# Second chunk's first layer ahead of the first chunk's second layer, with its activations in the room of v

## The chip, the core and the metric

The kernel runs on one core of a Trainium2 chip. Five engines work side by side, each through its own list of instructions in order: TensorE (PE in the profile; weight loads are PEld), VectorE (DVE), ScalarE (ACT), GpSimd (POOL) and SyncE (SP), which issues most transfers. The metric is the device time of one execution in microseconds.

## The reference

Block-sparse attention feeds a two-layer network. Cut to what matters:

```python
batch, n_heads, seq, head_dim = (4, 8, 768, 64)
block = 32                       # 24 blocks of keys, 3 random ones a row of blocks
mask  = neighbours (|i-j| <= 1) | first or last block row or column | 3 sampled blocks
scores = where(mask, q @ k.T / sqrt(64), -1e9)
attn = exp(scores - max); attn = attn / (sum + 1e-9)
x = (attn @ v)  -> 3072 tokens x 512
h = x @ w_in                     # 512 x 2048
g = where(h > 0, h, exp(min(h, 0)) - 1)
out = g @ w_out                  # 2048 x 512
```

All inputs and the output are float32.

## The kernel before

The 3072 tokens are 12 chunks of 256, three to a batch; t counts the chunks, b the batches. A chunk is made of two units of 128 tokens; the units of the first batch come in the order (0,1), (4,5), (2,3), those of the others (4,5), (0,1), (2,3). Unit 5 holds also the first and the last 32 tokens, which see all keys (the special rows, sp). Float32 values are kept as two float16 parts, hi and lo, and a product is taken as three float16 products.

For one chunk there is, first, attention: scores on TensorE (L479), the minimum on VectorE (L491), the exponential on ScalarE (L506), its hi part on ScalarE (L513) and lo part on VectorE (L518), a transposing transfer (L525), the product with v on TensorE (L538), normalisation on VectorE (L558), and transposes and splitting into xT (L340 on ScalarE, L343 on VectorE, one helper for q, k, v, p and x). Second, the first layer: eight pieces h{t}_{f} of 256 columns of w_in (`ffn_h`, L653), 24 matmuls each, and for each its activation: ScalarE L661 and L667, VectorE L671 (the last reader of the PSUM buffer), VectorE L675 (hi part of g), and the subtraction L678 (lo part of g), which is on VectorE for chunk 0 and on GpSimd for the others. Third, the second layer: o{t}_0 and o{t}_1 (`ffn_o`, L689), 48 matmuls each, scaled out by ScalarE (L697) and stored.

Buffers matter here. h and o share a pool of three PSUM buffers, so a fourth piece waits until the last reader of the first is done: L671 for an h, L697 for an o. The tile e of the activation has four buffers. The loads of q, k and v from memory share three staging buffers (tag st). The hi and lo parts of v of a batch lie in vN; they are stored to a scratch in memory (L418) from which the rows of each unit are gathered (SP L428 and L436, GpSimd L438). g lies in two tiles, gt, one set for all chunks.

The weights arrive as float32 and are decoded on the chip, in pieces: bits on ScalarE (L264, L267) and VectorE (L272, L275), the hi part on ScalarE (L287), the lo part on VectorE (L288). w_in (tiles wi) comes first and w_out (tiles wo) after; the last four pieces of w_out go through the small room wk, 512 columns at a time.

The order is set by a table of work: `st.at(step, rank, fn)` places each function; the steps are gone through from the first, by rank inside a step, and a scheduler that knows the tiles makes each engine's list of it. A chunk has 16 steps; `F0` = 12 is the first step of h0, `LEAD` = 22 the steps by which attention runs ahead of h. Chunk t has h at steps 12 + 16 t on and o eight steps after. `e0` is the step at which a chunk's attention starts; `unit`, `special`, `k_piece`, `v_piece` and `q_piece` place their work after it.

Of the kernel before, what the change touches and what calls it, by code (L numbers as in the profile page):

```python
# [13 lines left out]
ALU = mybir.AluOpType  # L14
# [25 lines left out]
def kernel(  # L40
# [26 lines left out]
    nc = tc.nc  # L67
# [15 lines left out]
    NFC = DFF // P  # L83
    NFP = NFC // 2
# [20 lines left out]
    st = Steps()  # L105
# [535 lines left out]

    hS, eS, oS = {}, {}, {}
    PROD_X = ((0, 0), (1, 0), (0, 1))
    gh, gl = ([gt[f // 4][:, f // 2 % 2, l, f % 2] for f in range(NFP)] for l in range(2))

    def ffn_h(t, f):
        ps = ps_f.tile([P, 2, CW], F32, tag="f", name=f"h{t}_{f}")
# [24 lines left out]
            e, hS.pop((t, f)), -IH * GS, e, op0=ALU.mult, op1=ALU.min)  # L672

    def ffn_act4(t, f):
        nc.vector.tensor_copy(gh[f], eS[t, f])  # L675

    def ffn_act5(t, f):
        (nc.gpsimd if t else nc.vector).tensor_tensor(  # L678
            gl[f], eS.pop((t, f)), gh[f], op=ALU.subtract)

    def ffn_o(t, m, part, nparts):
        if part == 0:
            oS[t, m] = ps_f.tile([P, DM], F32, tag="f", name=f"o{t}_{m}")
        o = oS[t, m]
        ms = slice(m * P, (m + 1) * P)
        for f in range(NFP * part // nparts, NFP * (part + 1) // nparts):
            for e in range(2):
                for n, (g, l) in enumerate(((gh, 0), (gh, 1), (gl, 0))):
                    nc.tensor.matmul(  # L689
                        o, lhsT=g[f][:, e, ms], rhs=wo[f // 2][:, f % 2, l, e],  # L690
                        start=(f == 0 and e == 0 and n == 0),
                        stop=(f == NFP - 1 and e == 1 and n == 2))

# [21 lines left out]
    NSTEP = 2 * NFP  # L715
    LEAD = 22
    F0 = 12

    def unit(s, b, u, qd, t, c0):
        lag = 4 if t == 1 else 6  # L720
        if qd == 0:
            st.at(s - (1 if t == 0 or s == F0 + 2 * NSTEP - LEAD else 3), 3.0,
                  lambda: gather_k(b, u, nc.scalar if t == 1 else nc.vector))
        st.at(s, 0, lambda: scores(b, u, qd))
        st.at(s, 5, lambda: sm_min(b, u, qd))
        st.at(s, 6, lambda: sm_exp(b, u, qd))
        if t == 0:
            st.at(s + 1, 0.5, lambda: turn_p(b, u, qd))
            st.at(s + 2, 1, lambda: attn_v(b, u, qd))
            if qd == 1:  # L730
                st.at(s + 2, 3.5, lambda: norm(b, u))
                st.at(s + 3, 0.6, lambda: turn_x(b, u, t, c0))
            return
        st.at(s + 1, 3.1, lambda: sm_hi(b, u, qd))
        st.at(s + 1, 3.2, lambda: sm_lo(b, u, qd))
        st.at(s + 2, 0.5, lambda: sm_T(b, u, qd))
        a = s + lag
        st.at(a, 1, lambda: attn_v(b, u, qd))
        if u == UL or qd == 1:
            st.at(a, 3.5, lambda: norm(b, u))  # L740
            st.at(a + 1, 7, lambda: turn_x(b, u, t, c0))

    def special(s, b, qd, t):
        st.at(s, 0, lambda: sp_scores(b, qd))
        for j in range(2):
            st.at(s, 5 + j, lambda j=j: sp_min(b, qd, j))
            st.at(s, 5.1 + j, lambda j=j: sp_exp(b, qd, j))
            st.at(s + 1, 3 + .3 * j, lambda j=j: sp_hi(b, qd, j))
            st.at(s + 1, 3.1 + .3 * j, lambda j=j: sp_lo(b, qd, j))
            st.at(s + 2, 0.5, lambda j=j: sp_T(b, qd, j))  # L750
        lag = 4 if t == 1 else 6
        st.at(s + lag, 1, lambda: sp_av(b, qd))
        if qd == NQ - 1:
            st.at(s + lag, 3.5, lambda: sp_x(b, t, P))
# [8 lines left out]
    def k_piece(s, b, c):  # L763
        staged.append((s, lambda: load_k(b, c)))
        st.at(s, 7.2, lambda: turn_k(b, c))
# [9 lines left out]
    for t, (b, us) in enumerate(chunks):  # L775
        f0 = F0 + t * NSTEP
        e0 = f0 - LEAD

        if t == 0:
            e0 = 0  # L780
            at, first = (1, 2, 3, 4), (1, 3)
        elif t == 1:
            e0 = f0 - NSTEP + 2
            at, first = (e0, e0 + 2, e0 + 3, e0 + 5, e0 + 6), (e0, e0 + 3)
        elif us[1] < UL:
            at, first = (e0, e0 + 4, e0 + 8, e0 + 12), (e0, e0 + 8)
        else:
            at, first = (e0, e0 + 3, e0 + 5, e0 + 8, e0 + 12), (e0, e0 + 5)
        if us[1] < UL:
            for n, s in enumerate(at):  # L790
                unit(s, b, us[n // 2], n % 2, t, P * (n // 2))
        else:
            unit(at[0], b, us[0], 0, t, 0)
            unit(at[1], b, us[0], 1, t, 0)
            special(at[2], b, 0, t)
            special(at[3], b, 1, t)
            unit(at[4], b, UL, 0, t, P + 64)
        for m, u in enumerate(us):
            s = first[m]
            if t == 0:  # L800
                continue
            q_piece(s - 3, b, u)

        opens = t == 0 or chunks[t - 1][0] < b
        for m, u in enumerate(us):
            s = e0 - 4 + 8 * m
            if t == 0:
                s = 2 * m
            elif t == 2 and m == 0:
                s += 3  # L810
            if opens:
                st.at(s, 0.2, lambda b=b, m=m, e=None if t or m else nc.gpsimd: edge_v(b, m, e))
            for i in range(blocks_in(u)):
                st.at(s + (i if t else 0), 0.3, lambda b=b, u=u, i=i: gather_v(b, u, i))
        if opens:
            st.at(at[0] - 1, 2.95, lambda b=b: ends_of_k(b))

        if opens and b + 1 < B:
            for n, (g, qd) in enumerate(PIECES):
                if t == 0:  # L820
                    k_piece(24 + 2 * n, b + 1, n)
                    v_piece(22 + 2 * n, b + 1, g, qd)
                else:
                    k_piece(e0 + (11, 15, 23, 31, 39, 41)[n], b + 1, n)
                    v_piece(e0 + (17, 19, 25, 27, 33, 35)[n], b + 1, g, qd)

        u = f0
        for f in range(NFP):
            st.at(u + f, 2, lambda t=t, f=f: ffn_h(t, f))
            st.at(u + f + 1, 2.1, lambda t=t, f=f: ffn_act1(t, f))  # L830
            st.at(u + f + 1, 2.5, lambda t=t, f=f: ffn_act2(t, f))
            st.at(u + f + 1, 2.8, lambda t=t, f=f: ffn_act3(t, f))
            st.at(u + f + 1, 2.85, lambda t=t, f=f: ffn_act4(t, f))
            st.at(u + f + 1, 2.9, lambda t=t, f=f: ffn_act5(t, f))
        u += NFP
        for m in range(2):
            for n in range(4):
                st.at(u + 4 * m + n, 2, lambda t=t, m=m, n=n: ffn_o(t, m, n, 4))
            st.at(u + 4 * m + 4, 2.2, lambda t=t, m=m: ffn_out(t, m))
# [6 lines left out]


    UNITS = ((0, 0), (0, 1), (1, 0), (1, 1))
    w_step = [2 + 2 * f // 3 for f, _, _ in WORK]

    def bits1(i):
        with tc.issue_after(exps[0, *UNITS[min(i, 4) - 1]].ins) if i else nullcontext():
# [76 lines left out]
```

## Time and profile before

| | us |
|---|---|
| median of three runs | 765.03 (763.87 to 766.48) |
| the profiled execution's own time | 759.88 |
| its span, first to last instruction | 758.2 |
| TensorE busy | 682.8 (90%) |
| VectorE busy | 460.6 (61%) |
| ScalarE busy | 404.5 (53%) |
| GpSimd busy | 192.9 (25%) |
| mean granted TensorE clock | 0.975 |

The share of busy time is over the whole span. A timeline row gives the start, the length, the engine, the line, the operation, what it writes and reads by the program's names, and in brackets how long the engine was idle just before it and what ended that. On the chain of waits each piece is either work or a wait that the next piece of work stood behind.

### The profile page before, as it was taken

How to read it: one execution, taken by the hardware profiler on the slowest of the kernel's cores; microseconds unless marked ns; L12 is line 12 of the kernel's file. 1: busy time of each engine (PE TensorE's matmuls, PEld its weight loads, DVE VectorE, ACT ScalarE, POOL GpSimd, SP SyncE). 2: the span in 40 equal slices, each digit the busy share in tenths (PEclk: the TensorE clock that was granted, in tenths of full speed). 3: DMA queues.
4: the chain of work that ended last, by engine and by line, in shares of the span. 5: the costliest groups of instructions: out<-in, count | busy, mean ns of one | idle time of the engine just before them, and what ended most of it. 6: DMA issues, size and time to landing. Idle time of an engine off the chain costs nothing.

```text
span 758.2 us, 30169 instructions
## 1 busy us (share of the span) xinstructions
PE 682.8 (90%) x12999; PEld 476.8 (63%) x12999; DVE 460.6 (61%) x1211; ACT 404.5 (53%) x838; POOL 192.9 (25%) x193
## 2 busy tenths in 40 slices
PE   1456777798899999999999999999999999999997
PEld 1344654466658758668568558578568577586673
DVE  2778998976755855736558547557467357454130
ACT  2568996655436656535545546446347265354240
POOL 1315001002413313315205104314314215122040
PEclk9997988899999999999999999999999999999999
DMA  9999948786887786686597485677686636531000
GB/s 204 330 292 289 278 131 214 165 209 166 201 174 163 138 176 126 167 164 142 123 182 179 114 196 155 123 159 156 125 170 128 128 45 141 128 72 29 29 1 29
DMA packets 200986, 116.33 MB, mean 153 GB/s; under 512 B 163092, under 2 KB 175508, under 8 KB 200852
## 3 DMA queue, kind: packets, MB, share of 16 engines
q1 hardware_dynamic: 188144, 89.41, 53.4%
q0 software_dynamic: 5824, 17.83, 8.6%
q10 hardware_dynamic: 6884, 7.15, 3.6%
q8 instruction: 102, 1.67, 0.9%
q14 instruction: 32, 0.26, 0.1%
HBM read 74.52 MB, written 12.58 MB: 115 GB/s over the span
## 4 chain that ended last, share of the span: by engine, by line
PE 67%; DMA 4%; ACT 4%; DVE 3%; issue 2%; DVEq 1%; SPq 0%; ACTq 0%
PE o L689 28%; PE h L653 26%; PE s L479 4%; PE av L538 4%; DMA stv<-in_v_dram 4%; ACT t L506 2%; PE spx L625 1%; PE sp L574 1%; PE qt L352 1%; PE kt L352 1%; ACT p L513 1%; PE xt L352 1%; DVE p L518 1%; DVE e L671 1%; ACT e L661 0%
## 5 line engine op out<-in xcount | busy, mean ns | idle before, releaser
L653 PE MATMUL h<-xT,wi 128*128 128x256 f16 x2304 | 266.5, 276 | 13.3 <-DVE e L671 11.5
L689 PE MATMUL o<-wo,g 128*128 128x512 f16 x1152 | 261.0, 382 | 1.9 <-ACT wo L287 1.8
L653 PEld LDWEIGHTS <-wi 128*128 128x128 f16 x2304 | 223.6, 99 | 46.0 <-issue 13.0
L689 PEld LDWEIGHTS <-g 128*128 128x128 f16 x1152 | 109.6, 98 | 131.2 <-issue 6.8
L678 POOL TENSOR_TENSOR g<-e,g 128x512 f16<-128x512 f32 x88 | 102.2, 1163 | 322.7 <-DVE g L675 297.8
L438 POOL DMA_INDIRECT vg<-scr,rix x88 | 84.4, 960 | 196.4 <-PE av L538 173.2
L506 ACT ACTIVATE t<-t,m 128x256 f32<-128x256 f32 x176 | 87.1, 496 | 68.0 <-DVE m L491 67.9
L671 DVE SCALAR_TENSOR_TENSOR e<-h,e 128x512 f32<-128x512 f32 x96 | 66.0, 687 | 53.6 <-ACT e L667 50.5
L661 ACT ACTIVATE e<-h 128x512 f32<-128x512 f32 x96 | 56.2, 587 | 55.2 <-PE h L653 51.6
L491 DVE CUSTOM_DVE_ANT_1 t<-s,mask 128x256 f32<-128x256 f32 x176 | 64.1, 417 | 16.1 <-PE s L479 16.1
L518 DVE SCALAR_TENSOR_TENSOR p<-t,p 128x1024 f16<-128x1024 f32 x40 | 48.8, 1219 | 40.4 <-ACT p L513 39.9
L667 ACT ACTIVATE e<-e,gs 128x512 f32<-128x512 f32 x96 | 69.2, 722 | 1.9
L479 PEld LDWEIGHTS <-qT 64*32 64x32 f16 x4224 | 41.1, 93 | 37.5 <-issue 34.0
L479 PE MATMUL s<-kR,qT 64*32 64x160 f16 x2112 | 48.4, 245 | 13.0 <-DVE kR L447 6.7
L447 DVE COPY kR<-kT 128x256 f16 x246 | 49.8, 246 | 11.7 <-issue 6.3
L538 PEld LDWEIGHTS <-pT 128*32 128x32 f16 x4224 | 41.9, 97 | 22.8 <-issue 16.0
L538 PE MATMUL av<-vg,pT 128*32 128x64 f16 x4224 | 48.0, 201 | 9.1 <-issue 4.7
L479 PE MATMUL s<-kT,qT 64*32 64x96 f16 x2112 | 44.7, 214 | 11.5 <-issue 5.8
L675 DVE CAST g<-e 128x512 f16<-128x512 f32 x96 | 48.8, 508 | 2.7
L697 ACT ACTIVATE r<-o 128x512 f32<-128x512 f32 x24 | 14.3, 594 | 53.8 <-PE o L689 53.8
L513 ACT ACTIVATE p<-t 128x1024 f16<-128x1024 f32 x40 | 42.2, 1056 | 1.1
L343 DVE SCALAR_TENSOR_TENSOR xT<-xt,xT 128x512 f16<-128x512 f32 (+1 forms) x28 | 16.1, 573 | 38.7 <-ACT xT L340 38.7
(108 smaller groups left out, 547.8 us busy)
## 6 DMA issues: line engine op xcount, KB each, us to landing
vg<-scr SPq DMA_DIRECT2D x88, 192.0 KB
scr<-vN SPq DMA_DIRECT2D x12, 512.0 KB
wo<-in_moe_w_in_dram SPq DMA_DIRECT2D x5, 1024.0 KB
out_dram<-r ACTq DMA_DIRECT2D x20, 256.0 KB
stq<-in_q_dram SPq DMA_DIRECT2D x18, 256.0 KB
stv<-in_v_dram SPq DMA_DIRECT2D x18, 256.0 KB
stk<-in_k_dram SPq DMA_DIRECT2D x18, 256.0 KB
wo<-in_moe_w_out_dram SPq DMA_DIRECT2D x4, 1024.0 KB
```

What stands on the lines that cost most here:

```text
L438: nc.gpsimd.indirect_dma_start(out=t[0:96, 1, i], out_offset=None, in_=scr[b], in_offset=bass.IndirectOffsetOnAxis(ap=rix[0:96, qb : qb + ...
L479: nc.tensor.matmul(ps[32 * n : 32 * n + 32, j, pp, c], lhsT=qT[b, u][js, ql, a, q0 : q0 + 32], rhs=m, start=(ql + kl + part == 0), stop=(q ...
L491: nc.vector.tensor_tensor_reduce(t[:, j, pp, :].rearrange("p (a b) -> p a b", b=BLOCK), ps[:, j, pp, :].rearrange("p (a b) -> p a b", b=BL ...
L506: exps[b, u, qd] = nc.scalar.activation(t[:, j, pp, :], t[:, j, pp, :], AF.Exp, bias=m[:, j, pp : pp + 1], scale=-1.0, accum_out=s[:, h : ...
L518: nc.vector.scalar_tensor_tensor(p[:, 1, :], tS.pop((b, u, qd)).rearrange("p j g k -> p (j g k)"), PS, p[:, 0, :], op0=ALU.mult, op1=ALU.s ...
L538: nc.tensor.matmul(o[32 * n : 32 * n + 32, 4 * qd + 2 * pp + j, :], lhsT=t[:, pl * 8 + (2 * j + pp) * 2 + ab, 32 * n : 32 * n + 32], rhs=v ...
L653: nc.tensor.matmul(ps[:, e, :], lhsT=wi[f][:, wl, cc, e, :], rhs=x[:, xl, cc, :], start=(n == 0), stop=(n == 3 * NCC - 1))
L661: nc.scalar.activation(e, hS[t, f], AF.Exp, scale=IH)
L667: nc.scalar.activation(e, e, AF.Relu, bias=gs_col, scale=-GS)
L671: nc.vector.scalar_tensor_tensor(e, hS.pop((t, f)), -IH * GS, e, op0=ALU.mult, op1=ALU.min)
L678: (nc.gpsimd if t else nc.vector).tensor_tensor(gl[f], eS.pop((t, f)), gh[f], op=ALU.subtract)
L689: nc.tensor.matmul(o, lhsT=g[f][:, e, ms], rhs=wo[f // 2][:, f % 2, l, e], start=(f == 0 and e == 0 and n == 0), stop=(f == NFP - 1 and e ...
```

## The change

The first layer of chunk 1 is done in two parts. Its pieces f = 0 to 5 (`GV` = 6) are placed eight steps earlier, at steps 20 to 25, where the second layer of chunk 0 was; that moves to steps 26 to 33, and f = 6 and 7 of chunk 1 follow at 34 and 35. The second layer of chunk 1 stays at 36. Since gt still holds chunk 0's g then, the six pieces of chunk 1's g are kept in vN, one piece in the room of one of its six blocks; so the six pieces of v of batch 1, which would be written there from step 22 on, are placed at steps 44 to 46. The later half of the decode of w_out is spread over steps 15 to 23 instead of 12 to 22. Chunk 1's attention starts at step 8 instead of 14, chunk 3's at 48 instead of 38 with the shorter lag that chunk 1 had, chunk 4's two steps later; the gathers and the loads of k, q and v around them are placed to match. The line numbers from the second layer on grow by nine: L653 becomes L662, L671 L680, L675 L684, L678 L687, L689 L698, L697 L706.

On TensorE, at the end of chunk 0's first layer; before, o0 follows, between attention of the units 5 and 2, and h1 comes after:

```order
L653 MATMUL h0_7_1969<-xT0_1006,wi7_86 128x256
...
L689 MATMUL o0_0_2221<-wo0_87,g0_91 128x512
...
L352 MATMUL qt0_3_2964<-ident_74,stq_0_3_2766 128x128 x4
L538 MATMUL av0_2_2977<-vg0_94,pT0_2_0_2634 32x64
...
L653 MATMUL h1_0_3074<-xT1_2388,wi0_79 128x256
```

and in the changed kernel:

```order
L390 MATMUL xt0_5_2511<-ident_74,xf0_5_2445 128x64 x4
L352 MATMUL qt0_2_2521<-ident_74,stq_0_2_1784 128x128 x4
...
L662 MATMUL h1_0_2534<-xT1_2149,wi0_79 128x256
...
L662 MATMUL h1_3_2768<-xT1_2149,wi3_82 128x256
...
L662 MATMUL h1_4_2810<-xT1_2149,wi4_83 128x256
...
L662 MATMUL h1_5_2851<-xT1_2149,wi5_84 128x256
...
L698 MATMUL o0_0_2981<-wo0_87,g0_91 128x512
```

The transposes of unit 5 (xt0_5) now stand ahead of h1, and h1_0 to h1_5 ahead of o0_0. The buffers turn in the order of allocation, so that o0_0 takes the one that h1_3 had.

On VectorE, the end of the decode of w_out (wk is the small room, wo3 the last tile of w_out, p and t attention of unit 2); before:

```order
L272 SCALAR_TENSOR_TENSOR wk_93<-wk_93 128x512 x2
L275 SCALAR_TENSOR_TENSOR wk_93<-wk_93 128x512 x2
L518 SCALAR_TENSOR_TENSOR p0_2_0_2627<-t0_2_0_2520,p0_2_0_2627 128x1024
L288 TENSOR_TENSOR wo3_90<-wk_93,wo3_90 128x512 x2
L638 SCALAR_TENSOR_TENSOR xT1_2388<-spx0_2273,xT1_2388 128x4x64
L555 TENSOR_SCALAR sum0_5_2262<-sum0_5_2262 128x4
L343 SCALAR_TENSOR_TENSOR vN_96<-stv_1_0_1_2020,vN_96 128x4x64
```

and in the changed kernel:

```order
L680 SCALAR_TENSOR_TENSOR e1_2_2793<-h1_2_2714,e1_2_2793 128x512
L684 CAST vN_96<-e1_2_2793 128x512
L272 SCALAR_TENSOR_TENSOR wk_93<-wk_93 128x512
...
L518 SCALAR_TENSOR_TENSOR p0_2_0_2799<-t0_2_0_2749,p0_2_0_2799 128x1024
...
L275 SCALAR_TENSOR_TENSOR wk_93<-wk_93 128x512
L680 SCALAR_TENSOR_TENSOR e1_3_2835<-h1_3_2768,e1_3_2835 128x512
L680 SCALAR_TENSOR_TENSOR e1_4_2876<-h1_4_2810,e1_4_2876 128x512
L288 TENSOR_TENSOR wo3_90<-wk_93,wo3_90 128x512
L684 CAST vN_96<-e1_3_2835 128x512
```

The activation of h1 now stands between the steps of the decode, and writes vN; the decode's last L288 stands behind L680 of e1_4. The work on xT1 from the special rows and on unit 5 has moved ahead of all this.

On ScalarE, around the start of chunk 2's first layer in the changed kernel (r is the scaled output, stv a staged piece of v):

```order
L706 ACTIVATE r1_0_3934<-o1_0_3764 128x512
...
L340 ACTIVATE vN_96<-stv_1_0_0_3807 128x4x2x64
L340 ACTIVATE vN_96<-stv_1_0_1_3809 128x4x2x64
L340 ACTIVATE vN_96<-stv_1_1_0_3823 128x4x2x64
...
L340 ACTIVATE vN_96<-stv_1_2_1_4093 128x4x2x64
L706 ACTIVATE r1_1_4009<-o1_1_3921 128x512
...
L670 ACTIVATE e2_0_4051<-h2_0_3984 128x512
```

Before, the first three of these v pieces stood ahead of r0_0 and the others around e1_0 and e1_1; now all six stand between r1_0 and r1_1.

The diff:

```diff
--- before.py
+++ after.py
@@ -641,7 +641,16 @@
 
     hS, eS, oS = {}, {}, {}
     PROD_X = ((0, 0), (1, 0), (0, 1))
-    gh, gl = ([gt[f // 4][:, f // 2 % 2, l, f % 2] for f in range(NFP)] for l in range(2))
+    PROD_O = ((0, 0), (0, 1), (1, 0))
+
+
+    GV = 6
+    gv = vN.rearrange("p n h l d -> p (n h l d)").rearrange(
+        "p (f l e t) -> p f l e t", f=GV, l=2, e=2)
+
+    def g_part(t, f, l):
+        return gv[:, f, l] if t == 1 and f < GV else gt[f // 4][:, f // 2 % 2, l, f % 2]
+
 
     def ffn_h(t, f):
         ps = ps_f.tile([P, 2, CW], F32, tag="f", name=f"h{t}_{f}")
@@ -672,11 +681,11 @@
             e, hS.pop((t, f)), -IH * GS, e, op0=ALU.mult, op1=ALU.min)
 
     def ffn_act4(t, f):
-        nc.vector.tensor_copy(gh[f], eS[t, f])
+        nc.vector.tensor_copy(g_part(t, f, 0), eS[t, f])
 
     def ffn_act5(t, f):
         (nc.gpsimd if t else nc.vector).tensor_tensor(
-            gl[f], eS.pop((t, f)), gh[f], op=ALU.subtract)
+            g_part(t, f, 1), eS.pop((t, f)), g_part(t, f, 0), op=ALU.subtract)
 
     def ffn_o(t, m, part, nparts):
         if part == 0:
@@ -685,9 +694,9 @@
         ms = slice(m * P, (m + 1) * P)
         for f in range(NFP * part // nparts, NFP * (part + 1) // nparts):
             for e in range(2):
-                for n, (g, l) in enumerate(((gh, 0), (gh, 1), (gl, 0))):
+                for n, (gl, l) in enumerate(PROD_O):
                     nc.tensor.matmul(
-                        o, lhsT=g[f][:, e, ms], rhs=wo[f // 2][:, f % 2, l, e],
+                        o, lhsT=g_part(t, f, gl)[:, e, ms], rhs=wo[f // 2][:, f % 2, l, e],
                         start=(f == 0 and e == 0 and n == 0),
                         stop=(f == NFP - 1 and e == 1 and n == 2))
 
@@ -715,11 +724,13 @@
     NSTEP = 2 * NFP
     LEAD = 22
     F0 = 12
+    SHORT = 1, 3
+    AFTER = F0 + 4 * NSTEP - LEAD + 2, F0 + 5 * NSTEP - LEAD
 
     def unit(s, b, u, qd, t, c0):
-        lag = 4 if t == 1 else 6
+        lag = 4 if t in SHORT else 6
         if qd == 0:
-            st.at(s - (1 if t == 0 or s == F0 + 2 * NSTEP - LEAD else 3), 3.0,
+            st.at(s - (1 if t == 0 or s in AFTER else 3), 3.0,
                   lambda: gather_k(b, u, nc.scalar if t == 1 else nc.vector))
         st.at(s, 0, lambda: scores(b, u, qd))
         st.at(s, 5, lambda: sm_min(b, u, qd))
@@ -748,7 +759,7 @@
             st.at(s + 1, 3 + .3 * j, lambda j=j: sp_hi(b, qd, j))
             st.at(s + 1, 3.1 + .3 * j, lambda j=j: sp_lo(b, qd, j))
             st.at(s + 2, 0.5, lambda j=j: sp_T(b, qd, j))
-        lag = 4 if t == 1 else 6
+        lag = 4 if t in SHORT else 6
         st.at(s + lag, 1, lambda: sp_av(b, qd))
         if qd == NQ - 1:
             st.at(s + lag, 3.5, lambda: sp_x(b, t, P))
@@ -779,10 +790,11 @@
         if t == 0:
             e0 = 0
             at, first = (1, 2, 3, 4), (1, 3)
-        elif t == 1:
-            e0 = f0 - NSTEP + 2
+        elif t in SHORT:
+            e0 = 8 if t == 1 else f0 - 12
             at, first = (e0, e0 + 2, e0 + 3, e0 + 5, e0 + 6), (e0, e0 + 3)
         elif us[1] < UL:
+            e0 += 2 * (t == 4)
             at, first = (e0, e0 + 4, e0 + 8, e0 + 12), (e0, e0 + 8)
         else:
             at, first = (e0, e0 + 3, e0 + 5, e0 + 8, e0 + 12), (e0, e0 + 5)
@@ -806,8 +818,12 @@
             s = e0 - 4 + 8 * m
             if t == 0:
                 s = 2 * m
-            elif t == 2 and m == 0:
-                s += 3
+            elif t == 1 or t == 4:
+                s = (5, 12)[m] if t == 1 else (55, 60)[m]
+            elif t == 3:
+                s = e0 + 2 * m
+            elif t == 5:
+                s += 2
             if opens:
                 st.at(s, 0.2, lambda b=b, m=m, e=None if t or m else nc.gpsimd: edge_v(b, m, e))
             for i in range(blocks_in(u)):
@@ -819,20 +835,25 @@
             for n, (g, qd) in enumerate(PIECES):
                 if t == 0:
                     k_piece(24 + 2 * n, b + 1, n)
-                    v_piece(22 + 2 * n, b + 1, g, qd)
+                    v_piece(F0 + 2 * NSTEP + n // 2, b + 1, g, qd)
+                elif t == 3:
+                    k_piece((49, 53, 61, 69, 77, 79)[n], b + 1, n)
+                    v_piece((58, 60, 63, 65, 71, 73)[n], b + 1, g, qd)
                 else:
                     k_piece(e0 + (11, 15, 23, 31, 39, 41)[n], b + 1, n)
                     v_piece(e0 + (17, 19, 25, 27, 33, 35)[n], b + 1, g, qd)
 
-        u = f0
+
+
         for f in range(NFP):
+            u = f0 - (NFP if t == 1 and f < GV else 0)
             st.at(u + f, 2, lambda t=t, f=f: ffn_h(t, f))
             st.at(u + f + 1, 2.1, lambda t=t, f=f: ffn_act1(t, f))
             st.at(u + f + 1, 2.5, lambda t=t, f=f: ffn_act2(t, f))
             st.at(u + f + 1, 2.8, lambda t=t, f=f: ffn_act3(t, f))
             st.at(u + f + 1, 2.85, lambda t=t, f=f: ffn_act4(t, f))
             st.at(u + f + 1, 2.9, lambda t=t, f=f: ffn_act5(t, f))
-        u += NFP
+        u = f0 + NFP + (GV if t == 0 else 0)
         for m in range(2):
             for n in range(4):
                 st.at(u + 4 * m + n, 2, lambda t=t, m=m, n=n: ffn_o(t, m, n, 4))
@@ -846,7 +867,7 @@
 
 
     UNITS = ((0, 0), (0, 1), (1, 0), (1, 1))
-    w_step = [2 + 2 * f // 3 for f, _, _ in WORK]
+    w_step = [2 + 2 * f // 3 if f < NFC else NFC - 1 + (f - NFC + 1) // 2 for f, _, _ in WORK]
 
     def bits1(i):
         with tc.issue_after(exps[0, *UNITS[min(i, 4) - 1]].ins) if i else nullcontext():
```

## The prediction

> **What bounds the kernel now.** I read the slices of the page first, then busy time by stages, then TensorE's timeline where it has gaps, then the chain of waits.
>
> ```profile
> PE   1456777798899999999999999999999999999997
> DVE  2778998976755855736558547557467357454130
> PEclk9997988899999999999999999999999999999999
> ```
>
> Each digit is 1/40 of 758.2 us. TensorE (PE) is full from slice 12 on, some 210 us in, and is filling up before. VectorE (DVE) is the other way round: nearly full in slices 3 to 9. The same by stages, cut where the second layer of chunk 0 (o0) starts, where o1 stands at its 25th matmul, and where the first layer of chunk 4 (h4) starts; columns are length, then busy time (count) of PE, PEld, DVE, ACT, POOL, then clock, DMA share, GB/s:
>
> ```profile
> 0.00:122.90 122.90, 68.95 (x1480) 53.05 (x1480) 93.92 (x202) 87.83 (x154) 23.62 (x33) 0.89 0.88 249
> 122.90:206.85 83.95, 71.57 (x1471) 48.27 (x1464) 65.27 (x170) 49.46 (x104) 18.59 (x18) 0.95 0.83 194
> 206.85:336.67 129.82, 129.43 (x2537) 87.59 (x2530) 80.06 (x230) 68.84 (x153) 35.62 (x35) 0.99 0.74 157
> 336.67:758.20 421.53, 412.83 (x7528) 287.90 (x7528) 221.41 (x611) 198.41 (x428) 115.05 (x108) 1.00 0.55 116
> ```
>
> Up to 206.85 us TensorE is idle for 206.85 - 68.95 - 71.57 = 66.3 us; from there to h4 for 0.4 us. So only the first 207 us can give anything, and a microsecond won there is won at the end unless a new gap opens: the orders of TensorE, VectorE and ScalarE from h4 on are the same in both kernels. Where the idle time ends, on TensorE's timeline:
>
> ```profile
> 88.20 7.07 PE L653 MATMUL h<-xT,wi 128*128 128x256 f16 x48 [3.88 <-DVE e L671]
> ...
> 104.75 0.58 PE L653 MATMUL h<-xT,wi 128*128 128x256 f16 x2 [4.69 <-DVE e L671]
> ...
> 122.90 5.83 PE L689 MATMUL o<-wo,g 128*128 128x512 f16 x25
> ...
> 206.85 6.29 PE L689 MATMUL o<-wo,g 128*128 128x512 f16 x24
> ```
>
> The first layer waits for L671 on VectorE, which frees its PSUM buffer (three are shared by h and o), while VectorE is busy decoding weights: that order, not TensorE's work, sets this stage.
>
> **The change, part by part.** I find the moment T0 at which o0 starts now, add the TensorE work left from there to h4, and compare with 336.67.
>
> *T0.* In the changed order o0 stands behind h1_0 to h1_5 and takes the PSUM buffer of h1_3, so it waits for L680 (old L671) of e1_3. That instruction stands near the end of the decode of w_out: only one L288 comes after it. Before, the last L288 ended here, with the small work behind it:
>
> ```profile
> 155.28 1.28 DVE L288 TENSOR_TENSOR wo<-wk,wo 128x512 f16<-128x512 f32 x2
> 156.48 0.41 DVE L638 SCALAR_TENSOR_TENSOR xT<-spx,xT 128x256 f16<-128x256 f32 x1
> 156.81 0.16 DVE L555 TENSOR_SCALAR sum<-sum 128x4 f32<-128x4 f32 x1
> 156.88 0.42 DVE L343 SCALAR_TENSOR_TENSOR vN<-stv,vN 128x256 f16<-128x256 f32 x1
> ...
> 159.62 0.42 DVE L558 TENSOR_TENSOR xf<-av,sum 128x256 f32<-128x256 f32 x1 [0.65 <-PE av L538]
> 160.90 0.29 DVE L343 SCALAR_TENSOR_TENSOR xT<-xt,xT 128x128 f16<-128x128 f32 x1 [0.86 <-ACT xT L340]
> ...
> 171.35 0.69 DVE L343 SCALAR_TENSOR_TENSOR kT<-kt,kT 128x512 f16<-128x512 f32 x1 [0.21 <-ACT kT L340]
> 171.96 0.69 DVE L671 SCALAR_TENSOR_TENSOR e<-h,e 128x512 f32<-128x512 f32 x1
> ...
> 176.87 0.42 DVE L675 CAST g<-e 128x512 f16<-128x512 f32 x1
> 177.21 0.42 DVE L343 SCALAR_TENSOR_TENSOR vN<-stv,vN 128x256 f16<-128x256 f32 x1
> ...
> 178.49 0.74 DVE L675 CAST g<-e 128x512 f16<-128x512 f32 x1
> ```
>
> The decode was done at 155.28 + 1.28 = 156.56. Rows that follow at once start about 0.08 us before the other ends (171.35 to 171.96 is 0.61, 176.87 to 177.21 is 0.34), so I count 0.61 for a 128x512 row, 0.34 for a cast. Comparing what stands ahead of L680 of e1_3 now with what stood ahead of that last L288: added are four L680 (4 x 0.61 = 2.4), three casts L684 (1.0), and chunk 0's last pieces, which were behind the decode: two xT of 0.2 net, one L638 (0.33), one L558 (0.33), the reciprocal pair (0.24), 1.3 in all. Gone are one L288 of 512 columns (0.6) and two lo parts of v, the old vN rows (2 x 0.34). Sum: 2.4 + 1.0 + 1.3 - 0.6 - 0.7 = +3.4. The work of the chunk's attention is the same on both sides, only its place differs.
>
> The subtraction of chunk 1 runs on GpSimd (POOL), and for e1_0 to e1_2 falls now into this stretch, beside decode work; before it came later:
>
> ```profile
> 177.79 1.15 POOL L678 TENSOR_TENSOR g<-e,g 128x512 f16<-128x512 f32 x1 [15.83 <-ACT e L667]
> ```
>
> The cast of 178.49, which stands beside it, took 0.74 instead of 0.42. The bounds are 0 (GpSimd meets only instructions that read PSUM) and 3 x 1.16 = 3.5 (it holds VectorE up for its whole length three times). I take 1.4: one full hold and one cast's 0.3, since the decode's instructions are closer to casts than to the rest. The Trainium skill, "SBUF — State Buffer", section "SBUF: two separate sides", says that VectorE operations in a two-port mode or with two SBUF inputs and GpSimd operations take one shared pair of ports as an exclusive lock, the loser waiting to the end. The decode's L288 has two SBUF inputs; by that rule the upper bound holds, and the sum below gets 2.1 us worse; the 0.74 beside 0.42 agrees with a wait but with less than a whole 1.15.
>
> So T0 = 156.56 + 3.4 + 1.4 = 161.4, with 158 to 165 around it: VectorE's own idle time may be more or less than before.
>
> *From T0 to h4.* TensorE's prices, from the chain that ended last, where it runs without a gap:
>
> ```profile
> 329.01 0.94 PE s L479 x84
> 329.94 5.29 PE o L689 x24
> 335.23 0.44 PE qt L352 x4
> 335.67 1.00 PE av L538 x96
> 336.67 5.35 PE h L653 x48
> ```
>
> (One piece of scores is 96 rows, of which some share their time with the row before; 0.94 is for the whole piece.) After T0 the changed kernel has everything that the old one had after 206.85, and besides: all of o0 and 24 matmuls of o1 (120 x 5.29 / 24 = 26.5), h1_6 and h1_7 (5.35), eight groups of transposes (8 x 0.44 = 3.5), three pieces of scores (2.8) and three of av (3.0): 41.1 us. The old stretch lasted 129.8; less its idle 0.4 and its slow first piece (6.29 against 5.29) 128.4. So h4 would come at 161.4 + 41.1 + 128.4 = 330.9 with no new gap. TensorE's own work before T0 is 68.95 + 71.57 - 41.1 = 99.4 us, which fits into 161.
>
> *What the gap costs on its own.* T0 follows on idle time, so the first rows run at a lower clock; the old one paid 1.0 for this at 206.85 and I take 1.0 (0 to 2).
>
> *v of batch 1.* vN holds chunk 1's g, so the six pieces of v are loaded and split only when o1 has read it. In the old kernel this lay beside o0 and h1, with these waits on the chain:
>
> ```profile
> 162.63 7.06 DMA stv<-in_v_dram
> 169.72 0.63 ACT vN L340
> ...
> 171.52 4.33 DMA stv<-in_v_dram
> ...
> 177.70 2.77 DMA stv<-in_v_dram
> ```
>
> Now they stand on ScalarE between r1_0 and r1_1, and r1_1 frees the PSUM buffer that h2_2 needs; behind them waits L670 of e2_0. A pair of pieces writes two of vN's six blocks, so the first pair waits until o1_1 has read two f's of g, the last until it has read six: 36 and 12 matmuls before o1_1's end at 5.29 / 24 = 0.22 each, some 8 and 2.6 us. Three pieces can be loaded early. The fourth takes the staging buffer of the first and the sixth that of the fourth, so two loads of length L follow one another: the first is split by some 7.3 us before o1_1's end, the fourth by 6.2 - L before it, the sixth lands 2 L - 6.1 after it, and with its hi part (0.63) and r1_1 (another 0.6) h2_2 can start at 2 L - 4.9. It is due after h2_0, h2_1 and one transpose, 5.35 + 0.44 = 5.8. So the loads cost nothing up to L = 5.3, and 3.4 us at 7.06. The three rows are 7.06, 4.33 and 2.77, mean 4.7, two of three below 5.3: I take 0.3. The store to memory and the gathers behind it have the eight pieces of h2 as cover (4 x 5.35 = 21.4 us) before av of unit 4 reads them; I cost them at nothing; without it every microsecond of delay would be one at that av.
>
> *v of batch 2, in front of h3.* The work table puts the third and fourth piece at steps 63 and 65 as before, but the first two at 58 and 60 instead of 55 and 57, with h3 from step 60, and in ScalarE's order pieces three and four with r2_1 now stand ahead of the last xT of chunk 3 (r2_1 stood behind it). h3_0 needs that xT. Two hi parts cost 1.26; a late load costs up to 4.33. Bounds 0 and 4.3; I take 1.2.
>
> Edits that cost nothing: the order of the three products in L698 is as before; g's room in vN has the shape of the old one; chunk 3's attention with the shorter lag is ten steps later, under TensorE's full stretch, where VectorE is busy 80.06 of 129.82 us; with that cover gone each wait would show as s or av rows after a gap.
>
> Sum: h4 at 330.9 + 1.0 + 0.3 + 1.2 = 333.4 against 336.67, a gain of 3.2 us. The span goes from 758.2 to 755.0; the profiled run (759.88, so 1.7 us around the span) to 756.7. The runs shown have a median of 765.03, 5.15 above the profiled run; I carry the difference over: 765.03 - 3.2 = 761.8.
>
> **Rivals.**
>
> *1. VectorE stops waiting.* In the old decode VectorE was not full:
>
> ```profile
> 100.00:120.00 20.00, 11.60 (x207) 8.29 (x208) 17.97 (x30) 18.50 (x35) 0.00 (x0) 0.75 0.71 188
> 120.00:140.00 20.00, 17.05 (x228) 8.63 (x223) 18.48 (x36) 11.04 (x15) 3.67 (x4) 0.91 0.77 183
> 140.00:160.00 20.00, 16.52 (x377) 9.88 (x376) 17.55 (x52) 14.84 (x34) 0.18 (x1) 0.83 0.78 171
> ```
>
> It idled 2.0 + 1.5 + 2.4 = 5.9 us. If the first layer's work fills these holes, T0 is near 155.5 and the time 761.8 - 5.9 = 755.9. For it: h1 gives VectorE work at any time. Against it: ScalarE's 18.50 of 20 says that it is as much the limit there, and h1 adds to it.
>
> *2. v is late (slower).* The room of v is free only after o1; if each of its loads takes 7.06, h2 waits 3.4 and h3 up to 4.3, 7.7 against the 1.5 taken: 761.8 + 6.2 = 768.0. It costs anything from 5.3 us a load, and turns the sign when both waits pass 4.7 together. For it the 7.06, and that the sixth load waits for the fourth; against it 4.33 and 2.77.
>
> *3. GpSimd holds VectorE up in full (no change).* Three full subtractions instead of 1.4: 2.1 us more, 763.9. The rule of the Trainium skill named above is this rival. For it: more instructions with two inputs from SBUF stand there than before; against it: 0.32 us on the one cast.
>
> **How the numbers follow.** 0.3% is 2.3 us, about what a measurement of this kernel can tell from no change. The forecast, 761.8, has a chance of 0.58 and a range of its own from 758.5 to 765.5, from T0's 158 to 165: 0.36 faster, 0.20 within 0.3%, 0.02 slower. Rival 1 has 0.12, all faster. Rival 2 has 0.13: 0.12 slower, 0.01 same. Rival 3 has 0.17: 0.02 faster, 0.13 same, 0.02 slower. Together faster 0.50, same 0.34, slower 0.16. The range leaves out about half of rivals 1 and 2: 756.5 to 767.5.
>
> **What would show it.** In the profile of the changed kernel: the first L698 at 158 to 165, released by DVE e L680; h4's first row at 331 to 336; no gap over 1 us between o0's start and h2_2; a cast or L288 beside POOL L687 longer than 0.42 or 0.69. The prediction is wrong if h2 or h3 waits for ACT r or xT by over 3 us (rival 2), if L698 starts before 157 (rival 1), or if TensorE waits between h1_0 and h1_5 for something other than VectorE, ScalarE's L670 say.

## The result, and the profile after

The changed kernel took 806.4 us (median; 801.71 to 810.64) beside 765.68 us for the one before: a ratio of 1.0555, with a 95% interval of 1.0492 to 1.0618. On another occasion it took 801.9 us beside 764.5, a ratio of 1.0497 (1.0454 to 1.0540). So it is some 5% slower, 37 to 41 us, where I had forecast a gain of 3. The profiled execution has a span of 799.6 us.

The slices of the changed kernel's page (1/40 of 799.6 us each):

```profile
PE   2454868679999777899999999999999999999998
DVE  3775978995527744473564855845656637355130
PEclk9655967799999999989999999999999999999999
```

TensorE is full in slices 10 to 13 and sinks again in 14 to 17 (260 to 340 us), where before it stayed full. VectorE has a hole in slice 4 (60 to 80 us) that it did not have. By stages, first the changed kernel, cut at the start of o0 (T0), of h2 and of h4:

```profile
0.00:174.90 174.90, 99.52 (x2167) 77.57 (x2168) 129.27 (x282) 114.22 (x207) 32.76 (x42) 0.75 0.85 214
174.90:233.07 58.17, 57.98 (x849) 32.38 (x848) 30.54 (x87) 23.21 (x52) 5.88 (x5) 0.97 0.44 100
233.07:378.76 145.69, 123.70 (x2457) 83.71 (x2455) 79.09 (x232) 69.12 (x154) 41.35 (x38) 0.94 0.74 166
378.76:799.60 420.84, 412.93 (x7537) 287.87 (x7528) 221.04 (x612) 198.51 (x428) 115.06 (x108) 1.00 0.55 116
```

and the kernel before, cut at the end of the decode of w_out, at h2 and at h4:

```profile
0.00:156.56 156.56, 96.18 (x1903) 67.80 (x1904) 124.26 (x273) 110.70 (x198) 27.29 (x37) 0.89 0.86 233
156.56:229.27 72.71, 66.37 (x1434) 45.06 (x1433) 46.85 (x140) 36.05 (x83) 18.79 (x18) 0.98 0.84 194
229.27:336.67 107.40, 107.40 (x2146) 76.06 (x2138) 68.12 (x189) 59.38 (x130) 31.76 (x30) 1.00 0.73 155
```

From h4 on both are alike (420.8 and 421.5 us). The loss is all ahead of h4, which comes at 378.76 instead of 336.67, and it has two parts. First, the start of o0:

```profile
175.09 4.44 PE L698 MATMUL o<-wo,g 128*128 128x512 f16 x12 [4.42 <-DVE e L680]
```

o0 waits for what I had named, but starts at 175.1, not at 161.4 as I had worked out: 13.7 us. Second, from o0 to h4 it takes 378.76 - 174.90 = 203.9 us instead of 172: 32 us, almost all of it behind h2, where TensorE had no idle time before and now has 145.69 - 123.70 = 22.0 us. In the profile of the other occasion (`after_again` below) o0 starts at 170.2 and h4 at 379.8, so there the two parts are 8.8 and 37.6 us: the sum is nearly the same, its division varies.

The gaps behind h2 on TensorE's timeline, of which these are some:

```profile
290.61 0.25 PE L479 MATMUL s<-kR,qT 64*32 64x160 f16 x5 [3.77 <-issue]
...
312.14 7.19 PE L662 MATMUL h<-xT,wi 128*128 128x256 f16 x48 [3.30 <-ACT xT L340]
...
333.63 2.79 PE L662 MATMUL h<-xT,wi 128*128 128x256 f16 x24
...
339.42 4.45 PE L662 MATMUL h<-xT,wi 128*128 128x256 f16 x24 [2.99 <-DVE e L680]
```

Most belong to the attention of chunks 3 and 4 or to what waits for it. The longer ones also cost behind themselves: the same 24 matmuls of h take 4.45 us after the last of these gaps and 2.79 us before it.

### The profile page after: what moved, and what is told of

Same layout as the page of the kernel before. It is cut to its first block, busy times and chain, and to the rows that moved or that the text cites. A ratio compares the mean times of both kernels' runs of the same rounds, so it can differ in the third digit from the quotient of the medians.

```text
span 799.6 us, 30149 instructions
## 1 busy us (share of the span) xinstructions
PE 694.1 (87%) x12999; PEld 481.5 (60%) x12999; DVE 459.9 (58%) x1211; ACT 405.1 (51%) x838; POOL 195.0 (24%) x193
## 5 line engine op out<-in xcount | busy, mean ns | idle before, releaser
L662 PE MATMUL h<-xT,wi 128*128 128x256 f16 x2304 | 272.2, 279 | 12.1 <-DVE e L680 5.9
L662 PEld LDWEIGHTS <-wi 128*128 128x128 f16 x2304 | 226.7, 100 | 47.9 <-issue 13.3
L698 PE MATMUL o<-wo,g 128*128 128x512 f16 x1080 | 248.8, 387 | 4.4 <-DVE e L680 4.4
L698 PEld LDWEIGHTS <-g 128*128 128x128 f16 x1080 | 103.9, 99 | 127.6 <-issue 13.1
L687 POOL TENSOR_TENSOR g<-e,g 128x512 f16<-128x512 f32 x82 | 95.7, 1169 | 328.6 <-DVE g L684 285.0
L438 POOL DMA_INDIRECT vg<-scr,rix x88 | 86.1, 978 | 196.1 <-PE av L538 175.7
L680 DVE SCALAR_TENSOR_TENSOR e<-h,e 128x512 f32<-128x512 f32 x96 | 65.8, 687 | 52.9 <-ACT e L676 47.1
L447 DVE COPY kR<-kT 128x256 f16 x246 | 46.6, 236 | 20.8 <-PE s L479 13.0
L706 ACT ACTIVATE r<-o 128x512 f32<-128x512 f32 x24 | 14.2, 594 | 69.8 <-PE o L698 69.8
L684 DVE CAST g<-e 128x512 f16<-128x512 f32 x90 | 46.8, 521 | 2.6
```

The costliest lines, as they stand in the source:

```text
L438: nc.gpsimd.indirect_dma_start(out=t[0:96, 1, i], out_offset=None, in_=scr[b], in_offset=bass.IndirectOffsetOnAxis(ap=rix[0:96, qb : qb + ...
L662: nc.tensor.matmul(ps[:, e, :], lhsT=wi[f][:, wl, cc, e, :], rhs=x[:, xl, cc, :], start=(n == 0), stop=(n == 3 * NCC - 1))
L680: nc.vector.scalar_tensor_tensor(e, hS.pop((t, f)), -IH * GS, e, op0=ALU.mult, op1=ALU.min)
L687: (nc.gpsimd if t else nc.vector).tensor_tensor(g_part(t, f, 1), eS.pop((t, f)), g_part(t, f, 0), op=ALU.subtract)
L698: nc.tensor.matmul(o, lhsT=g_part(t, f, gl)[:, e, ms], rhs=wo[f // 2][:, f % 2, l, e], start=(f == 0 and e == 0 and n == 0), stop=(f == NF ...
```

## The experiments

Four theories are tried. A: the loss has two places, early attention and transfers ahead of the decode, and chunk 3's attention squeezed in front of h3. B: the core of the change, h1 ahead of o0, is the loss. From the second group on, C: the steps of chunk 3's attention stand too close together; and D: the late v of batch 1 is the loss.

### The change taken apart

`late_v` is the kernel before with v of batch 1 late and chunk 3's attention moved as in the change:

```diff
-            e0 = f0 - NSTEP + 2                      # t == 1 only, lag 4
+            e0 = 14 if t == 1 else f0 - 12           # t == 1 and t == 3, lag 4
-                    v_piece(22 + 2 * n, b + 1, g, qd)
+                    v_piece(F0 + 2 * NSTEP + n // 2, b + 1, g, qd)
                     ...
```

> The kernel before with one part of the change alone: v of batch 1 placed at steps 44 to 46, and chunk 3's attention, gathers and loads moved late and close together as in the change. Theory A (the cost lies in two places: transfers queued behind gathers and transposes early on, and chunk 3's attention squeezed in front of its first layer): TensorE as before until o1, then 20 to 32 us of gaps before h4, time 785 to 797. Theory B (the cost lies in the first layer of chunk 1 standing ahead of o0, tied to the decode on VectorE): 765 to 773, since the late v costs at most the 7.7 us that I had bounded.

`early_attn` is the kernel before with chunk 1's attention early:

```diff
-            e0 = f0 - NSTEP + 2
+            e0 = 8
+            elif t == 1:
+                s = (5, 12)[m]
                     ...
```

> The kernel before with chunk 1's attention and its gathers early as in the change, and nothing else. Theory A: the loads of weights stand behind gathers in SyncE's queue, h0 starts at 80 to 84 us instead of 72.84, time 772 to 780. Theory B: attention is only moved, 763 to 767.

`no_h` is the change without its core:

```diff
-        return gv[:, f, l] if t == 1 and f < GV else gt[f // 4][:, f // 2 % 2, l, f % 2]
+        return gt[f // 4][:, f // 2 % 2, l, f % 2]
-            u = f0 - (NFP if t == 1 and f < GV else 0)
+            u = f0
                     ...                         # o0 and the decode back at their old steps
```

> The change without its core: chunk 1's first layer stays behind o0, its g in the usual tiles and the decode at its old steps, while both attentions and v stand as in the change. Theory A: 795 to 812, about as slow as the change. Theory B: under 775.

Beside 764.23 us for the kernel before: `late_v` 788.57 (ratio 1.0321, 1.0276 to 1.0367), `early_attn` 771.3 (1.0068, 1.0039 to 1.0097), `no_h` 794.81 (1.0387, 1.0346 to 1.0428). The two parts add up: 24.3 + 7.1 = 31.4, and both together cost 30.6. All three came out near theory A (two of them less than 1 us below its ranges) and away from B. `no_h` has no h1 ahead of o0 and loses most of what the change loses. What is left for the core (h1 ahead of o0, its g in vN and the spread decode) is the distance from `no_h` to the changed kernel: 37.4 - 30.6 = 6.8 us by the medians of the second occasion, 10 by the first. Not the gain of 3 that I gave it.

### Chunk 3: v or attention

`squeezed_only` undoes one half of `late_v`: v of batch 1 is loaded where it was before.

```diff
-                    v_piece(F0 + 2 * NSTEP + n // 2, b + 1, g, qd)
+                    v_piece(22 + 2 * n, b + 1, g, qd)
```

> The kernel before, with chunk 3's attention, gathers and the loads around them late and close together as in the change, but v of batch 1 where it was. Theory C (TensorE waits because the steps of chunk 3's attention stand too close for their chain across engines): from h2 to h4 125 to 142 us instead of 107.3, time 780 to 795. Theory D (v's own lateness, its loads, stores and gathers, is what costs): from h2 to h4 under 115 us, time 762 to 770.

788.69 us (1.0302, 1.0257 to 1.0346), as slow as `late_v`. The late v costs nothing, and theory D is out; the attention of chunk 3 moved behind it costs the 24 us, together with what was moved along with it: gathers, loads, and chunk 4's attention, which is two steps later. The stretch from h2 to h4 in `squeezed_only`, in `lag_only` and in `close_early` (both below), in that order:

```profile
224.86:369.10 144.24, 122.77 (x2458) 84.00 (x2456) 77.23 (x228) 68.98 (x152) 33.74 (x30) 0.94 0.59 130
```

```profile
235.97:355.06 119.09, 109.50 (x2137) 77.39 (x2136) 67.79 (x191) 60.60 (x132) 32.74 (x30) 0.96 0.64 139
```

```profile
245.07:353.32 108.25, 105.50 (x1929) 74.67 (x1921) 61.96 (x173) 54.09 (x120) 31.90 (x30) 0.98 0.63 143
```

Idle time of TensorE there: 21.5, 9.6 and 2.8 us, and none in the kernel before. Of the 21.5 us, 14.9 lie ahead of h3 and 6.6 behind its start, among these 2.8 and 2.1 in front of two av of chunk 4; in `lag_only` and `close_early` under 0.2 us lies behind the start of h3.

`lag_only` gives chunk 3 the short lag at its old place, `close_early` the short lag and the close steps at its old place:

```diff
-        lag = 4 if t == 1 else 6
+        lag = 4 if t in (1, 3) else 6                # lag_only and close_early
-        elif t == 1:
-            e0 = f0 - NSTEP + 2
+        elif t in (1, 3):                            # close_early
+            e0 = f0 - NSTEP + 2 if t == 1 else e0
```

> The kernel before, with four steps instead of six between scores and av in chunk 3's attention and nothing else. If the short lag makes TensorE wait for the chain through VectorE, ScalarE and the transposes: 8 to 20 us of gaps between h2 and h3, time 772 to 785. If the lag is long enough: 763 to 768.

> The kernel before, with chunk 3's attention as close together as in the change (steps 0, 2, 3, 5, 6 and a lag of four) but still from step 38, ten steps ahead of where the change has it. If closeness and lag cost the 24 us of the squeezed kernel: 780 to 790. If what costs is that the attention ends right in front of h3 (no slack, so each delay is TensorE's): 763 to 770.

775.41 us (1.0118, 1.0067 to 1.0168) and 774.41 (1.0137, 1.0097 to 1.0177), beside 763.97. So the short lag costs some 11 us on its own by the medians, the closeness adds nothing to the time, and the late place, with what was moved along, has the rest, some 13 us. Of theory C the short lag holds, then, and the closeness of the pieces does not show. But equal times are not equal waits: in `close_early` TensorE idles 12.2 us between the end of the decode and h2 (10.6 in `lag_only`, 6.3 in the kernel before), so more than half of its added idle time lies ahead of h2. Both expectations of `close_early` were off: it lies between them. Where the lag bites is one row of TensorE in `lag_only`:

```profile
254.88 0.48 PE L625 MATMUL spx<-spT,vN 128*64 128x64 f16 x10 [8.39 <-DMA spT<-spp]
```

The special rows' transposed probabilities are not there four steps after their scores. In SyncE's queue the second of the two transposes stands here behind four gathers (it is issued at 244.35, they from 242.32 on), in the kernel before ahead of them; so the short lag and the order of that queue can both be in this wait, and no run parts them.

Two tries to mend it inside the changed kernel. `spread` puts chunk 3's attention at steps 44 to 52 with the long lag. (In it the transposed probabilities of unit 4's first half are overwritten before av reads them; the work is the same.) `turns_first` puts the gathers for chunk 4's first unit behind the transposes of the special rows, and asks for the gathers of both units two or three steps later:

```diff
+            if t == 3:                               # spread
+                at, first = (44, 46, 48, 50, 52), (44, 48)
                     ...
+                    with tc.issue_after(turns[1, 1, 1].ins) if late else nullcontext():   # turns_first
+                        gather_v(b, u, i)
```

> The changed kernel with chunk 3's attention spread over steps 44 to 52 and six steps between scores and av instead of four, its gathers where they were. Theory C: TensorE's idle time from h2 to h4 falls from 22 us to 8 to 14, time 790 to 798. Theory D: 802 to 808.

> The changed kernel with the four gathers for chunk 4's first unit put behind the transposes of chunk 3's special rows in SyncE's queue. If those transposes are slow because 768 KB of gathers stand ahead of them (8.65 us at issue): they go out within 3 us, time 797 to 802. If they are slow for another reason: 803 to 810.

801.11 us (1.0470) and 802.05 (1.0490), against the changed kernel's 801.9 (1.0497): no gain from either that can be told from the spread; both expectations for `spread` failed. In `turns_first` the two transposes took 1.43 and 2.19 us at their issue instead of 3.75 and 4.12 in the change, so the gathers ahead of them did slow them; but 2.6 us passed between the two, and a wait turned up at a later step (xt for xf, 3.96 us). With the long lag (`spread`) the last av still stands right in front of h3. So neither a later gather nor a longer lag alone gives the time back while the attention has to be done between v's arrival and h3.

### Ahead of o0

VectorE's waits from 60 us to T0 in the changed kernel, and to the end of the decode in the kernel before (sum, times, longest):

```profile
DVE qT L343 <- ACT qT L340: 5.0, 1, 5.0
DVE spm L599 <- ACT spt L592: 4.3, 2, 4.1
DVE spp L607 <- ACT spp L602: 2.6, 2, 2.4
DVE wo L288 <- ACT wo L287: 2.4, 3, 1.4
```

```profile
DVE wo L288 <- ACT wo L287: 2.3, 3, 1.2
DVE xf L558 <- PE av L538: 1.7, 1, 1.7
DVE qT L343 <- ACT qT L340: 1.5, 1, 1.5
```

The new ones are steps of chunk 1's attention: its q (ScalarE stands ready for the q of unit 4 and waits for TensorE, with the decode queued behind) and the special rows. `early_loads` asks for the weights earlier, `q_later` moves that q two steps, `repaired` does both and takes over `turns_first`; `sub_on_vector` has the subtraction of h1's first six pieces on VectorE; `after_again` is the changed kernel:

```diff
-            st.at(max(w_step[last] + 1, s - 4), 1.9, lambda i=i: load_w(i))
+            st.at(max(w_step[last] + 1, s - 8), 1.9, lambda i=i: load_w(i))        # early_loads
-            at, first = (...), (e0, e0 + 3)
+            at, first = (...), (e0 + 2 * (t == 1), e0 + 3)                         # q_later
-        (nc.gpsimd if t else nc.vector).tensor_tensor(
+        (nc.gpsimd if t > 1 or t == 1 and f >= GV else nc.vector).tensor_tensor(   # sub_on_vector
```

> The changed kernel with the loads of the weights' later pieces asked for eight steps ahead of their decode instead of four, so that several stand ahead of gathers and transposes in SyncE's queue. Theory A: h0 starts some 5 to 10 us sooner than the 82.5 of the change and o0 at 160 to 168 instead of 175, time 792 to 800. Theory B: the order on VectorE sets o0's start, 804 to 808.

> The changed kernel with the subtraction of h1's first six pieces on VectorE instead of GpSimd. If GpSimd holds VectorE up for its whole length (rival 3 of the prediction): VectorE gains 3.5 us of holds and pays 2 us of its own before o0, time 803 to 805. If the holds are short: 807 to 811.

> The changed kernel with the q of unit 4 loaded and transposed two steps later, so that ScalarE does its hi part behind two more pieces of the decode. If the one wait of 5.0 us (VectorE for qT, ScalarE for TensorE) is what makes the decode late: h0 starts 2 to 5 us sooner, o0 at 170 to 173, time 2 to 5 us under the changed kernel's on this chip. If other waits take its place: within 1.5 us of it.

> The changed kernel with three repairs together: q of unit 4 later, weight loads asked for eight steps ahead, the transposes of the special rows ahead of the gathers. If late transfers and single waits are the loss before o0: o0 at 163 to 168, time 790 to 797. If the loss is that many steps of attention stand between the steps of the decode: o0 at 168 to 173, 798 to 803.

> The changed kernel itself beside the others, for a difference on one chip: 801 to 809.

802.74 us (1.0495), 805.77 (1.0533), 804.57 (1.0570), 793.23 (1.0402, 1.0352 to 1.0451) and 801.9 (1.0497, 1.0454 to 1.0540). The first three cannot be told from the changed kernel. In `early_loads` h0 starts at 78.6 and o0 at 170.3, as in `after_again` (78.9 and 170.2); so theory A's reason for the first place, loads of weights queued behind gathers, is not borne out on its own. In `q_later` h0 starts at 75.2 instead of 78.9 to 82.5, but o0 at 173.8: other waits took the place (special rows, 4.4 and 4.0). Only the three repairs together help, by 8.7 us; o0 starts at 167.0. Where they help is not settled: beside the first profile of the changed kernel h2 starts 7.4 us sooner and h4 7.8, beside `after_again` h2 starts 2.5 us sooner and h4 8.8. VectorE up to the end of the decode in `early_attn`, `no_h`, `after_again` and `repaired`:

```profile
0.00:168.50 168.50, 96.45 (x2098) 68.36 (x2099) 127.29 (x283) 110.44 (x200) 28.13 (x39) 0.81 0.89 227
```

```profile
0.00:166.31 166.31, 97.79 (x2098) 69.68 (x2099) 125.37 (x279) 109.66 (x199) 28.44 (x39) 0.77 0.88 226
```

```profile
0.00:171.42 171.42, 99.47 (x2171) 77.25 (x2172) 130.15 (x285) 115.24 (x209) 36.30 (x42) 0.79 0.85 220
```

```profile
0.00:167.54 167.54, 95.64 (x2181) 73.95 (x2182) 129.07 (x284) 115.35 (x209) 32.64 (x42) 0.79 0.86 225
```

Idle: 41.2, 40.9, 41.3 and 38.5 us, against 32.3 in the profile of the kernel before. The execution profiled there was a short one (759.88 us, where the median was 765): `squeezed_only`, `lag_only` and `close_early`, whose edits come later than this stage, have 34.9, 34.9 and 36.6 us, and their decode ends at 159.1, 158.9 and 161.1 instead of 156.56. So the early attention alone puts 4 to 9 us of idle time into the decode, with or without h1 ahead of o0; in the time of `early_attn` it is 7.1 us.

### The other way

`late_attn` moves chunk 1's attention two steps later (its special rows then read some of v of the next batch; the work is the same); `before_early_loads` and `before_loads_12` are the kernel before with weight loads asked for 8 and 12 steps ahead:

```diff
-            e0 = f0 - NSTEP + 2
+            e0 = f0 - NSTEP + 4                                                    # late_attn
-            st.at(max(w_step[last] + 1, s - 4), 1.9, lambda i=i: load_w(i))
+            st.at(max(w_step[last] + 1, s - 8), 1.9, lambda i=i: load_w(i))        # s - 12
```

> The kernel before, with chunk 1's attention two steps later (from 16 instead of 14), the other way from the change. If attention placed early takes VectorE's and ScalarE's time from the decode (7 us for six steps): 1 to 3 us faster, 761 to 763. If not: 764 to 768.

> The kernel before, with the later loads of the weights asked for eight steps ahead of their decode instead of four. If VectorE's idle time in the decode (32 us up to its end) comes from late loads: 2 to 5 us faster, 759 to 762. If it comes from waits between the engines: 763 to 767.

> The kernel before with the later loads of the weights asked for twelve steps ahead instead of four (eight gave a ratio of 0.9963). If the gain comes from loads that were late: 759 to 762. If the first pieces are now held up: 763 to 767.

766.09 us (1.0022, 0.9988 to 1.0055): no difference, so the price of attention's place is not a slope that goes on the other way. 761.52 (0.9963, 0.9939 to 0.9987) beside 763.97, and 761.77 (0.9963, 0.9935 to 0.9991) beside 764.5: a small gain, the same for both, 0.4%, within the expectations for late loads. In their traces VectorE idles 33.7 and 32.6 us up to the end of the decode, between the 32.3 and the 36.6 named above, so where the gain lies is not shown. These two are faster than both kernels of this case.

## Why the prediction was wrong

**T0: the work was right, the idle time was not.** I had VectorE's work ahead of o0 grow by 3.4 + 1.4 = 4.8 us; it grew from 124.26 to 129.27, by 5.0. But its idle time grew from 32.3 to 45.6, by 13.3 us, where I had said that idle time "may be more or less than before" and given the step 158 to 165. (By the spread named above, 5 to 11 us of the 13.3 are the change's: 41.3 and 45.6 against 34.9 to 36.6. The rest may lie in the short execution whose profile I built on.) The sentence that failed is "The work of the chunk's attention is the same on both sides, only its place differs". A moved step takes its waits with it: attention is a chain over four engines and the transfer queue, and in an engine's list what stands behind a waiting step waits too. By the runs that base had to be the end of the decode with early attention, 166.3 (`no_h`) or 168.5 (`early_attn`) instead of 156.56; with 4.8 on top that gives 171.1 or 173.3, and the two executions of the changed kernel have 175.1 and 170.2.

**From T0 to h4: "edits that cost nothing" cost most.** I put chunk 3's attention at nothing, since it would lie "under TensorE's full stretch". It lay there before only because it ran ten steps ahead of its use. Moved to steps 48 to 54 with four steps of lag it ends right in front of h3, so each wait in it is TensorE's: `squeezed_only`, which has this move and what goes with it, loses 24.5 us. The prediction named the sign, s or av rows after a gap, and such rows came; what it left out was any price for them. The quoted prices of TensorE held; they were added up for a TensorE that never waits. Of the 32 us, 22.0 are idle time against the 1.5 I had taken (v, and h3), and most of the rest is the clock behind the gaps (0.94 over the 145.69 us from h2 to h4 is some 8.7 us of it), for which I had taken 1.0 once.

**v of batch 1: right.** I took 0.3 for h2; there is no gap ahead of h2_2, and `squeezed_only` equals `late_v`. The gathers behind it, which I had put at nothing, show as 0.95 us in front of one av (263.83). Rival 2 had this as the way to a loss; its other place is there, on ScalarE ahead of h3 in the changed kernel:

```profile
306.09 0.63 ACT L340 ACTIVATE vN<-stv 128x512 f16<-128x512 f32 x1 [7.20 <-DMA stv<-in_v_dram]
310.80 0.63 ACT L340 ACTIVATE vN<-stv 128x512 f16<-128x512 f32 x1 [4.09 <-DMA stv<-in_v_dram]
311.34 0.58 ACT L706 ACTIVATE r<-o 128x512 f32<-128x512 f32 x1
311.82 0.27 ACT L340 ACTIVATE xT<-xt 128x128 f16<-128x128 f32 x1
```

The last xT waits behind two late pieces of v of batch 2, and h3 for 3.30 us: inside my bounds of 0 to 4.3, above the 1.2 taken, and above the 3 us that I had named as the sign of rival 2. It is 3 us of the 42, not rival 2's 6 to 8.

**GpSimd beside VectorE: right in kind.** Of the three subtractions ahead of T0, in the changed kernel one held VectorE up; GpSimd first, VectorE below:

```profile
162.40 1.53 POOL L687 TENSOR_TENSOR vN<-e,vN 128x512 f16<-128x512 f32 x1 [22.12 <-DVE vN L684]
...
166.98 1.16 POOL L687 TENSOR_TENSOR vN<-e,vN 128x512 f16<-128x512 f32 x1 [0.93 <-DVE vN L684]
```

```profile
162.22 0.68 DVE L275 SCALAR_TENSOR_TENSOR wk<-wk 128x512 int32<-128x512 int32 x1
...
166.99 1.70 DVE L272 SCALAR_TENSOR_TENSOR wk<-wk 128x512 int32<-128x512 int32 x1
```

The L272 that started with a subtraction took 1.70 instead of 0.69, 1.0 more; the subtraction that started 0.18 us after an L275 took 1.53 instead of 1.16. In these two pairs whoever comes second takes longer by about as much as the other still had to run: 1.0 us of 1.15, and 0.37 of 0.50. The Trainium skill, "SBUF — State Buffer", section "SBUF: two separate sides", says just that of the shared ports, and these rows agree. Rival 3's price was too high, because the second and the third hold did not come about; `sub_on_vector`, which lies between its two expectations, shows no difference.

**Rival 1** (VectorE stops waiting) did not come about: h1 gave VectorE more to do, but filled no holes that can be seen (41.3 and 45.6 us idle with it, 40.9 and 41.2 with the early attention alone). None of the rivals had the loss, since all of them, as the forecast, left the attention's moves out.

**What stays open.** The 13 us between short lag and late place were not told apart: the gaps ahead of h3, the one for e of h3 and those in front of chunk 4's av are seen, but no run moves chunk 3's attention to its late place without chunk 4's and the gathers. Nor is it shown by which way the core costs its 7 us. g of chunk 1 in a room of its own, with chunk 3's attention where it was, would separate the core from what it brought along; it was not tried, and would take 12 KB more in each partition.

## What to carry over

When a change moves a chain of small steps, count the distance to their use, not only their work: compare steps of slack before and after, and price each lost step as a possible stall of the engine that was full. Such a chain in an engine's list in front of the critical work brings in its waits, and mending one of them lets the next one show. When one edit needs others (a room freed late, attention moved to suit), time these others alone first: here they lost 31 us, and the core had little to win.

## What was not expected of the hardware

The clock behind a short gap. TensorE's stretch ahead of the gap at 336.4 us and behind it, in the changed kernel:

```profile
330.00:336.40 6.40, 6.40 (x145) 5.50 (x144) 3.25 (x12) 4.02 (x12) 1.21 (x2) 1.00 0.39 122
339.42:343.87 4.45, 4.45 (x26) 3.37 (x26) 4.14 (x6) 1.61 (x3) 3.54 (x4) 0.62 0.97 205
```

A gap of 2.99 us was enough for a granted clock of 0.62 over the next 4.45 us, a price of 4.45 - 2.79 = 1.7 us on top of the gap. The Trainium skill, "TensorE: Matmul & The Clock Gate", Part 1, gives an idle window of about 3.4 us for this; here a shorter gap did it, and the same part says that the window runs free, so that its phase varies.

The length of one gap does not decide. Behind 1.90 us of idle time at 355.25 the clock is 0.65 over the next 4.75 us, behind 1.49 us at 274.62 it stays at 1.00 over 4.40. In stretches of 3.41 us, all counted from the same drop, TensorE is busy for 0.42, 1.20 and 1.51 us in those from 336.18, 288.39 and 353.25, and each time the next stretch has a clock of 0.50; in those from 284.98 and 271.33 it is busy for 1.86 and 1.92 us, and the clock stays at 1.00. Two gaps of 1.37 and 0.95 us close together (ahead of 262.67 and 263.83) were enough as well: busy for 1.09 us in the stretch from 261.09, then 0.50. So in this trace short gaps close together can cost as much clock as one long one.
